# Gated attention and a token/channel mixer on one core: diagonal score blocks from 10 of 16 tiles, score runs of three, and DMA and buffer times in the planner

## The chip, the core and the metric

The kernel runs on one core of one Trainium2 chip. A core has TensorE (matmuls, with its own queue of weight loads), VectorE, ScalarE, GpSimd and SyncE; each takes its instructions in order, and they wait for one another by semaphores. DMAs are issued from SyncE's and GpSimd's queues here and carried out by 16 shared DMA engines. The metric is device time in microseconds. The core's span in the profile (first to last instruction) is a little shorter than that time.

## The reference

For each of 8 batches (sequence S = 3008, width 256, score width 64):

```python
scores = (1.0 / S) * np.matmul(z, z.transpose(0, 2, 1))
attn = np.maximum(scores, 0.0) ** 2
x = u * np.matmul(attn, v)
h = np.maximum(x.transpose(0, 2, 1) @ w_tok1, 0.0) @ w_tok2   # w_tok1 3008x256
y = x + h.transpose(0, 2, 1)
out = y + np.maximum(y @ w_ch1, 0.0) @ w_ch2                  # w_ch1 256x1536
```

Scores are z times its own transpose, so `attn` is symmetric: tile (k, q) is the transpose of tile (q, k). Inputs and output are float32; the kernel works in bf16 with float32 sums.

## The kernel before

**Tiles.** The sequence is cut into 24 key tiles of 128 rows (the last has 64 real rows, held twice), and both sequence axes into six blocks of four tiles (`NQ`, `NG`): 512 columns, the last 448. A score block (b, q, g) is four key tiles by one row block: 16 tiles of 128x128. `zT` holds z transposed, twice, in partitions 0 to 63 and 64 to 127, so that two score matmuls of 64 rows run side by side on the two halves of TensorE's array.

**Scores.** The unit of work is half a score block, two key tiles (`units`, L237). `score_run` (L314) issues one pair of matmuls for each unit into one PSUM slot `sc`; `relu` (L337) has ScalarE write relu(scale x scores) to a buffer `at`; `square` (L358) has VectorE square it in place. There are six `at` buffers, and three PSUM slots (the `ring`), which the mixer's products share.

**Symmetry.** In batch 0 all 36 blocks are computed. In batches 1 to 7 only blocks with g >= q are; for g > q, `flip` (L374) has SyncE issue one DMA transpose of all 16 tiles into a buffer `fl`, which serves as block (b, g, q). The `at` buffer is counted free by the planner (`release`, L382) when both uses are over, the flip's use being over when it is issued. Diagonal blocks (g = q) are computed in full, although each is symmetric in itself.

**Attention times v.** `Block`, `next_half` and `do_half` (L458) go through the six blocks of a row block, in two halves of 128 output columns each (`acc0`, `acc1`). For the half-filled last key tile the two halves run side by side as a pair of 64-row matmuls (`do_tails`, L435). `gate` (L492) multiplies by u, transposed by DMA (`turn_u`, L164), and `turn_x` (L514) transposes the result by DMA for the token mixer.

**The mixer** of a batch runs during the next batch's attention, as `Piece`s: `tok1` (L539, sums over the sequence, into PSUM tile `a_ps`), `tok2` (L559), `ch1` (L583, twelve hidden tiles by two, each evacuated by ScalarE or VectorE) and `ch2` (L617, twelve matmuls a piece; two pieces share a PSUM slot, the first opens it and the second closes it). `residual` (L635) adds on VectorE and SyncE stores the rows.

**What sets the order.** The order of every queue is written out by a planner in Python, in the same program. It keeps a clock for TensorE (`pe`), and for each of `act`, `dve` and `sp` the time from which it is free; `push` (L251) queues an operation with its busy time and its latency, `run_engines` (L269) issues those that could have started. The main loop (L819) picks what TensorE does next: a run of score units, a half of attention times v, or a mixer piece. A run of scores wants as many PSUM slots at once as it has units; `most` (L827) is three, or two while a mixer piece has a slot open. Modelled costs: 0.92 us for ScalarE on a pair, 0.61 for VectorE, 2.45 busy and 6.5 to landing for a flip, 1.25 and 5.5 for x and u transposes of the mixer. Changing TensorE between full and 64-row matmuls is priced at 0.095 us (`on_pe`, L290). `can_score` allows a unit if the number of live `at` buffers permits it.

**Loads** are hung on steps of attention times v by `at_group` (L748): z, v and u of what comes next and, in batch 0, the weights. They go through GpSimd's queue. u's transpose (`turn_u`) and z's (`turn_next_z`, L740) go through SyncE's; the planner counts 1.25 us of SyncE for z's and nothing for u's.

Of the kernel before, what the change touches and what calls it, by code (L numbers as in the profile page):

```python
# [13 lines left out]
P = 128  # L14
QW = 512
GK = 4
# [26 lines left out]
def kernel(  # L43
# [52 lines left out]
    def load_z(b, c):  # L96
        zs = sb.tile([P, GK, d_qk], BF16, tag="zs", name="zs", bufs=6)
        n = full_tiles[c]
        nc.gpsimd.dma_start(out=zs[:, :n, :], in_=rows_of(z[b], c))
        if n < GK:  # L100
            for r in range(2):
                nc.gpsimd.dma_start(
                    out=zs[r * TAIL:(r + 1) * TAIL, n, :], in_=last_rows(z[b]))
        return zs

    def turn_z(zs, zT, c, engine, tag="zr", bufs=2):
# [38 lines left out]
    def load_v(b, c):  # L145
        vt = sb.tile([P, GK, D], BF16, tag="v", name="v_sb", bufs=8)
        n = full_tiles[c]
        nc.gpsimd.dma_start(out=vt[:, :n, :], in_=rows_of(v[b], c))  # L148
        if n < GK:
            for r in range(2):  # L150
                nc.gpsimd.dma_start(
                    out=vt[r * TAIL:(r + 1) * TAIL, n, :], in_=last_rows(v[b]))
        vs[b, c] = vt

    def load_u(b, q):
        ur = sb.tile([P, QW // P, D], BF16, tag="ur", name="ur", bufs=2)
# [5 lines left out]
        urs[b, q] = ur  # L162

    def turn_u(b, q):  # L164
        ur = urs.pop((b, q))
        uT = sb.tile([P, QW // P, DT, P], BF16, tag="uT", name="uT", bufs=3)
        nc.sync.dma_start_transpose(
            out=uT.rearrange("p t h s -> p (t h) s"),
            in_=ur.rearrange("p t d -> p (t d)"))
        uTs[b, q] = uT  # L170

    def load_w_tok1(c):
        n = full_tiles[c]
        nc.gpsimd.dma_start(
            out=w_tok1_sb[:, c * GK:c * GK + n, :], in_=rows_of(moe_w_tok1, c))
        if n < GK:
            nc.gpsimd.memset(w_tok1_sb[TAIL:, KT - 1, :], 0.0)
            nc.gpsimd.dma_start(
                out=w_tok1_sb[:TAIL, KT - 1, :], in_=last_rows(moe_w_tok1))

    def load_w_tok2(c):
# [5 lines left out]
        ws[c] = st  # L187

    def order_w_tok2(c):
        st = ws.pop(c)  # L190
# [9 lines left out]
    def load_w_ch(part):  # L200
        if part < 2:
            nc.gpsimd.dma_start(
                out=w_ch1_sb[:, part, :], in_=moe_w_ch1[part * P:(part + 1) * P, :])
        else:
            h = CHT // 2
            c0 = (part - 2) * h
            nc.gpsimd.dma_start(
                out=w_ch2_sb[:, c0:c0 + h, :],
                in_=moe_w_ch2.rearrange("(cc c) d -> c cc d", c=P)[:, c0:c0 + h, :])

# [30 lines left out]

    free = {"act": 0.0, "dve": 0.0, "sp": 0.0}
    waiting = {"act": [], "dve": [], "sp": []}
    ring = [Done(0.0) for _ in range(3)]
    live = {"at": 0, "fl": 0, "xT": 0, "x": 0, "h2": 0, "us": 0}
    ROOM = {"at": 6, "fl": 10, "xT": 9, "x": 7, "h2": 8, "us": 2}
    FAR = 1e9

    def push(engine, ready, busy, lat, fn, first=0, room=(), done=None):  # L251
        op = Op(ready, busy, lat, fn, first, room, done)
# [16 lines left out]
    def run_engines(until):  # L269

        while True:
            best = next_op()
            if best is None or best[0][0] > until:
                return
            (start, _, _), e, op = best
            waiting[e].remove(op)
            free[e] = start + op.busy
            op.done.t = start + op.lat
            op.fn(op.done.t)

    def known(*events):
# [8 lines left out]
    def on_pe(start, kind, length):  # L290
# [4 lines left out]
        pe[0] = start + length  # L295
        return start, pe[0]


    ats, ready_at = {}, {}
    turned = {}  # L300
# [13 lines left out]
    def score_run(us, start):  # L314
        slots = sorted((d for d in ring if d.t is not None), key=lambda d: d.t)
        for unit in us:
            (b, q, g), pr = unit
            zT = zTs[b].rearrange("p t s -> p (t s)")
            W = widths[q]
            slot = slots.pop(0)  # L320
            ring.remove(slot)
            begin = max(start, slot.t, known(turned[b, q], turned[b, g]))
            begin, start = on_pe(begin, "half", column_time(W))
            sc = psum.tile([P, 2, QW], F32, tag="ps", name="sc", bufs=3)
            for r in range(2):
                k = g * GK + pr * 2 + r
                h = slice(r * d_qk, (r + 1) * d_qk)
                nc.tensor.matmul(  # L328
                    sc[:, r, :W], zT[h, k * P:(k + 1) * P], zT[h, q * QW:q * QW + W],
                    start=True, stop=True)  # L330
            if pr == 0:
                live["at"] += 1
            done = push("act", begin + 0.43, 0.92, 1.08,
                        lambda t, unit=unit, sc=sc: relu(unit, sc, t))
            ring.append(done)

    def relu(unit, sc, t):  # L337
        (b, q, g), pr = unit
        W = widths[q]
        if pr == 0:  # L340
            ats[b, q, g] = sb.tile([P, GK * QW], BF16, tag="at", name="at", bufs=ROOM["at"])
            ready_at[b, q, g] = []
        at = ats[b, q, g]
        pair = slice(2 * pr, 2 * pr + 2)
        if g > q and b > 0:

            view = at.rearrange("p (j i s) -> p j i s", i=GK, s=P)[:, :, pair, :]
            sv = sc.rearrange("p i (j s) -> p j i s", s=P)
        else:
            view = at.rearrange("p (i w) -> p i w", w=QW)[:, pair, :W]  # L350
            sv = sc[:, :, :W]
        nc.scalar.activation(view, sv, ACT.Relu, scale=inv_S)  # L352
        ready_at[b, q, g].append(
            push("dve", t, 0.61, 0.75, lambda t: square(unit, view, t)))
# [3 lines left out]
    def square(unit, view, t):  # L358
# [12 lines left out]
            attn = at.rearrange("p (i w) -> p i w", w=QW)  # L371
        blocks[b, q, g] = (Done(t), attn, "at", uses)

    def flip(b, q, g, at, uses, done):  # L374
        fl = sb.tile([P, GK, QW], BF16, tag="fl", name="fl", bufs=ROOM["fl"])
        live["fl"] += 1
        nc.sync.dma_start_transpose(
            out=fl.rearrange("p j (i s) -> p (j i) s", s=P), in_=at[:])
        blocks[b, g, q] = (done, fl[:, :, :], "fl", [1])
        release("at", uses)  # L380

    def release(name, uses):  # L382
        uses[0] -= 1
        if not uses[0]:
            live[name] -= 1


    class Block:
# [30 lines left out]
    def finished(blk, g):  # L419
        blk.parts[g] -= 1  # L420
        if not blk.parts[g]:
            _, _, name, uses = blocks.pop((blk.b, blk.q, g))
            release(name, uses)

    def block_ready(blk, g):
        e = blocks.get((blk.b, blk.q, g))
# [105 lines left out]
    def add_mixer(b):  # L532
# [134 lines left out]
                               lambda end, q=q: tok2(q, end)))  # L667
        def add_ch1(q, c2):
            h2_done[q, c2] = Done()
            tails.append(Piece(4 * column_time(widths[q]), [u_done[q]],  # L670
                               lambda end: ch1(q, c2, end),
                               room=("h2", "us") if c2 == 0 else ("h2",)))

        def add_ch2(q, half, i):
            tails.append(Piece(1.312, [h2_done[q, c2] for c2 in range(CHT // 2)],
                               lambda end: ch2(q, half, i, end), opens=i == 0, closes=i == 1))


# [58 lines left out]
    load_u(0, 0)  # L737
    load_u(0, 1)

    def turn_next_z(b, c, zs):  # L740
        turn_z(zs, zTs[b + 1], c, nc.gpsimd)
        free["sp"] = max(free["sp"], pe[0]) + 1.25
        turned[b + 1, c] = Done(pe[0] + 9.0)


# [47 lines left out]
    for c in range(NG):  # L793
        at_group(NG + 1 + 4 * c, lambda c=c: load_w_tok1(c))
        at_group(NG + 3 + 4 * c, lambda c=c: load_w_tok2(c))
        at_group(NG + 6 + 4 * c, lambda c=c: order_w_tok2(c))
    for part in range(4):
        at_group(2 * NG + 6 * part, lambda part=part: load_w_ch(part))
# [20 lines left out]
    while cur[0] is not None or heads or tails:  # L819
# [4 lines left out]
        blk = cur[0]  # L824


        most = 2 if opened[0] is not None else 3  # L827
        n = can_score(done_units, most)
        slots = sorted(d.t for d in ring if d.t is not None)
        n_now = min(n, len(slots))  # L830
        ts = FAR
        if n_now:
            at = max(t, known(*(turned[b, c] for (b, q, g_), _ in
                                units[done_units:done_units + n_now] for c in (q, g_))))
            ts = max([at] + [slots[i] - 0.1 - 0.216 * i for i in range(n_now)])
# [75 lines left out]
```

## Time and profile before

| what | value |
|---|---|
| time, median of 7 runs | 1190.19 us (1189.67 to 1196.6) |
| the profiled execution's own time | 1189.89 us |
| its span | 1188.1 us |
| TensorE busy | 1169.5 us, 98% |
| ScalarE, VectorE busy | 551.8 us (46%), 539.1 us (45%) |
| SyncE's DMA queue (q1), share of 16 DMA engines | 54.8% |
| GpSimd's DMA queue (q0) | 19.4% |
| flips issued, and other DMA transposes | 105, and 188 (48 u, 48 x, 48 mixer, 44 z) |

Busy time is the union of an engine's instructions. A TensorE row shows source line, output <- inputs, rows*columns of the array used (64*128 is one half of it), then partitions x elements. "Idle before" is how long an engine stood still before a group, with what ended the wait; a wait for several things is put down to the last. An instruction on SyncE's queue is not counted as busy; its duration is the issue of a DMA, and "landing" is from its start to the last completion. A DMA share above 1 means that transfers queue up.

### The profile page before, as it was taken

What the parts mean: (1) busy time and instruction counts of PE and PEld (TensorE: products, weight loads), DVE (VectorE), ACT (ScalarE), POOL (GpSimd) and SP (SyncE); (2) the same over time, 40 slices, a digit from 0 to 9 for tenths busy, and PEclk for the clock granted to TensorE, in tenths of its full rate; (3) what the DMA queues carried; (4) which work ended last, traced back from release to release, by engine and by line L of the source; (5) the groups of instructions that cost most, each with busy time, mean ns of one, the idle gap of its engine ahead of it and who ended that gap; (6) DMA issues with size and microseconds to landing.
All of it is one profiled execution on the core that took longest, in us unless ns stands there. A gap on an engine that the chain in (4) does not pass through costs nothing.

```text
span 1188.1 us, 17216 instructions
## 1 busy us (share of the span) xinstructions
PE 1169.5 (98%) x6998; PEld 632.0 (53%) x7091; DVE 539.1 (45%) x727; ACT 551.8 (46%) x577; POOL 145.9 (12%) x272
## 2 busy tenths in 40 slices
PE   8998999999999999999999999999999999999998
PEld 3334554654546545565455555455454654555666
DVE  5774643355443453425534255243642336512444
ACT  7886464426533264424635436344454445523222
POOL 2660011010011010110101101011011000000000
PEclk9999999999999999999999999999999999999999
DMA  8999667995598884997659976699757967542121
GB/s 144 168 175 197 122 116 139 179 156 107 109 163 149 148 137 103 158 187 128 118 103 172 153 126 121 132 164 150 141 101 135 192 125 132 106 104 47 52 80 61
DMA packets 437311, 157.46 MB, mean 133 GB/s; under 512 B 401200, under 2 KB 414832, under 8 KB 437232
## 3 DMA queue, kind: packets, MB, share of 16 engines
q1 hardware_dynamic: 409376, 123.66, 54.8%
q0 software_dynamic: 27344, 32.32, 19.4%
q8 instruction: 55, 0.90, 0.3%
q10 hardware_dynamic: 512, 0.38, 0.1%
q14 instruction: 24, 0.20, 0.1%
HBM read 65.40 MB, written 24.64 MB: 76 GB/s over the span
## 4 chain that ended last, share of the span: by engine, by line
PE 96%; ACT 1%; issue 1%; DMA 1%; DVE 1%; DVEq 0%; ACTq 0%
PE acc L415 41%; PE op L626 21%; PE hp L595 20%; PE sc L328 7%; PE a_ps L548 4%; PE h_ps L565 3%; ACT at L352 1%; DMA fl<-at 1%; DVE xT L571 0%; DMA zf<-in_z_dram 0%; PE zp L134 0%; DVE h2pre L610 0%; PE wp L142 0%; DVE zr L128 0%; DVE at L360 0%
## 5 line engine op out<-in xcount | busy, mean ns | idle before, releaser
L352 ACT ACTIVATE at<-sc 128x1024 bf16<-128x1024 f32 (+1 forms) x366 | 346.8, 1017 | 289.1 <-PE sc L328 280.6
L360 DVE TENSOR_TENSOR at<-at 128x1024 bf16<-128x1024 bf16 (+1 forms) x366 | 255.4, 702 | 295.8 <-ACT at L352 291.9
L415 PE MATMUL acc<-at,v_sb 128*128 128x512 bf16 (+3 forms) x1440 | 351.9, 378 | 1.5 <-issue 0.3
L415 PEld LDWEIGHTS <-v_sb 128*128 128x128 bf16 (+1 forms) x2304 | 210.6, 98 | 264.4 <-issue 62.8
L608 ACT ACTIVATE h2pre<-hp 128x1024 bf16<-128x1024 f32 (+1 forms) x198 | 198.2, 1004 | 313.9 <-PE hp L595 313.9
L626 PE MATMUL op<-w_ch_sb,h2pre 128*128 128x256 bf16 (+1 forms) x2304 | 273.9, 273 | 0.1
L595 PE MATMUL hp<-xT,w_ch_sb 128*128 128x512 bf16 (+1 forms) x1114 | 267.6, 374 | 2.3 <-DVE xT L571 0.4
L626 PEld LDWEIGHTS <-h2pre 128*128 128x128 bf16 (+1 forms) x2304 | 224.0, 98 | 57.3 <-issue 11.6
L415 PE MATMUL acc<-fl,v_sb 128*128 128x512 bf16 (+1 forms) x818 | 198.5, 370 | 1.4 <-issue 0.5
L595 PEld LDWEIGHTS <-w_ch_sb 128*128 128x128 bf16 x1152 | 112.6, 98 | 128.6 <-issue 1.3
L639 DVE TENSOR_TENSOR res<-op,u_sb 128x512 f32<-128x512 f32 x88 | 60.6, 689 | 151.9 <-PE op L626 151.9
L610 DVE TENSOR_SCALAR h2pre<-hp 128x1024 bf16<-128x1024 f32 (+1 forms) x90 | 108.8, 1208 | 42.6 <-PE hp L595 42.6
L504 DVE TENSOR_TENSOR xT<-acc,uT 128x512 bf16<-128x512 f32 (+1 forms) x96 | 63.4, 665 | 137.5 <-PE acc L415 127.6
L328 PE MATMUL sc<-zT 64*128 64x512 bf16 (+1 forms) x732 | 103.7, 379 | 1.9 <-DMA zT<-zr 0.9
L158 POOL DMA_DIRECT2D ur<-in_u_dram x48 | 26.0, 543 | 361.1 <-DMA uT<-ur 354.3
L110 POOL COPY zr<-zs 128x512 bf16<-128x512 bf16 x42 | 29.1, 692 | 290.2 <-DMA zT<-zr 289.5
L328 PEld LDWEIGHTS <-zT 64*128 64x128 bf16 x732 | 29.6, 94 | 58.4 <-issue 42.1
L571 DVE TENSOR_TENSOR xT<-xT,h_ps 128x1024 bf16<-128x1024 bf16 (+1 forms) x48 | 55.5, 1190 | 7.0 <-PE h_ps L565 7.0
L548 PE MATMUL a_ps<-x_sb,w_tok_sb 128*128 128x256 bf16 x384 | 46.9, 278 | 4.9 <-ACT at L352 4.9
L148 POOL DMA_DIRECT2D v_sb<-in_v_dram x48 | 25.8, 541 | 190.9 <-PE acc L415 190.7
L548 PEld LDWEIGHTS <-w_tok_sb 128*128 128x128 bf16 x384 | 37.5, 100 | 16.2 <-issue 9.0
L565 PE MATMUL h_ps<-w_tok_sb,a_sb 128*128 128x512 bf16 (+1 forms) x183 | 44.7, 374 | 0.6
(35 smaller groups left out, 115.7 us busy)
## 6 DMA issues: line engine op xcount, KB each, us to landing
out_dram<-res SPq DMA_DIRECT2D x88, 256.0 KB, 2.4
v_sb<-in_v_dram POOLq DMA_DIRECT2D x40, 256.0 KB, 4.9
ur<-in_u_dram POOLq DMA_DIRECT2D x40, 256.0 KB, 5.6
zs<-in_z_dram POOLq DMA_DIRECT2D x35, 64.0 KB, 3.9
fl<-at SPq DMA_TRANSPOSE x105, 4.5
v_sb<-in_v_dram POOLq DMA_DIRECT2D x8, 192.0 KB, 6.5
w_ch_sb<-in_moe_w_ch_dram POOLq DMA_DIRECT2D x4, 384.0 KB, 6.3
ur<-in_u_dram POOLq DMA_DIRECT2D x8, 192.0 KB, 3.6
```

The source lines that it names most:

```text
L328: nc.tensor.matmul(sc[:, r, :W], zT[h, k * P:(k + 1) * P], zT[h, q * QW:q * QW + W], start=True, stop=True)
L352: nc.scalar.activation(view, sv, ACT.Relu, scale=inv_S)
L360: nc.vector.tensor_mul(view, view, view)
L415: nc.tensor.matmul(o, vs[blk.b, g][rows, i, dh * P:(dh + 1) * P], rhs, start=first, stop=stop, skip_group_check=True)
L504: nc.vector.tensor_mul(xT[:, dh, :full * P].rearrange("p (t s) -> p t s", s=P), acc[:, :full * P].rearrange("p (t s) -> p t s", s=P), uT[: ...
L548: nc.tensor.matmul(st["a_ps"][:, th, :], w_tok1_sb[:, k, th * P:(th + 1) * P], x[:, :, i, :], start=(k == 0 and th == 0), stop=(k == KT - ...
L565: nc.tensor.matmul(h[:, dh, :W], st["a"][:, th, dh * P:(dh + 1) * P], w_tok2_sb[:, th, q * QW:q * QW + W], start=(th == 0), stop=(th == 1))
L595: nc.tensor.matmul(hp[:, r, :W], w_ch1_sb[:, dc, cc * P:(cc + 1) * P], xT[:, dc, :W], start=(dc == 0), stop=(dc == DT - 1))
L608: nc.scalar.activation(h2[:, :, :W], hp[:, :, :W], ACT.Relu)
L610: nc.vector.tensor_single_scalar(h2[:, :, :W], hp[:, :, :W], 0.0, AX.max)
L626: nc.tensor.matmul(op[:rows[i], i, :], st["h2", q, cc // 2][:, cc % 2, c0:c0 + rows[i]], w_ch2_sb[:, cc, :], start=(cc == 0 and i == 0), s ...
L639: nc.vector.tensor_add(res.rearrange("p i (h d) -> p i h d", d=P), op.rearrange("p i (h d) -> p i h d", d=P), us[:, :, half * 2:half * 2 + ...
```

## The change

1. **Diagonal blocks of batches 1 to 7.** Key tile i of a diagonal block is multiplied with columns from i x 128 on only: 512, 384, 256 and 128 columns, 10 tiles of 16. The first unit takes tiles 0 and 1 (one on each half of the array); the second takes 2 and 3, with tile 2 on the half that had tile 1. Each tile then has its own activation and its own square. Three DMA transposes on SyncE (three tiles, two, one) mirror what lies above the diagonal into the same `at` buffer: the first two after the square of the first unit, the last after that of the second. The block is ready when the planner's time for the last has passed.
2. **Score runs.** A run is three units, with an open mixer piece or without (`RING`); if scores are wanted and a mixer piece has a slot open, the closing piece goes first.
3. **`at` buffers by time.** `at_free` holds the planned time from which each buffer is free: the landing of its flip or the end of its last product with v. A run of scores is not planned to start more than 0.6 us ahead of the time when the buffers it needs are free.
4. **DMA sharing in the planner.** Each load adds 1.3 us (parts of it, or more, by size) to a time up to which loads are under way (`loading`); a transpose that falls into it takes up to twice as long (`shared`). u's transposes now count 1.25 us on SyncE (`on_sp`), z's 0.6.
5. **Weights of the channel mixer.** `ch1` and `ch2` pieces also need `w_done`, 16 us after their load was asked for.

```diff
         vs[b, c] = vt
+        loading(LOAD)
...
         uTs[b, q] = uT
+        on_sp(1.25)
...
+    def loading(us):
+        loads[0] = max(loads[0], pe[0] + 1.0) + us
+
+    def shared(start, us):
+        both = min(us, max(0.0, loads[0] - start))
+        loads[0] += both
+        return us + both
...
+    at_free = [0.0] * ROOM["at"]
+    RING = 3
...
-            free[e] = start + op.busy
-            op.done.t = start + op.lat
+            extra = shared(start, op.busy) - op.busy if e == "sp" else 0.0
+            free[e] = start + op.busy + extra
+            op.done.t = start + op.lat + extra
...
+    def triangle(b, q, g):
+        return q == g and b > 0
+
+    def parts(unit):
+        (b, q, g), pr = unit
+        if not triangle(b, q, g):
+            return [(r, 2 * pr + r, 0, widths[q]) for r in range(2)]
+        order = ((0, 0), (1, 1)) if pr == 0 else ((1, 2), (0, 3))
+        return [(r, i, i * P, QW) for r, i in order]
...
-            begin, start = on_pe(begin, "half", column_time(W))
+            cost = column_time(W)
+            if triangle(b, q, g):
+                cost = (column_time(QW), column_time(P))[pr]
+            begin, start = on_pe(begin, "half", cost)
...
-            for r in range(2):
-                k = g * GK + pr * 2 + r
+            for r, i, c0, c1 in parts(unit):
+                k = g * GK + i
                 h = slice(r * d_qk, (r + 1) * d_qk)
                 nc.tensor.matmul(
-                    sc[:, r, :W], zT[h, k * P:(k + 1) * P], zT[h, q * QW:q * QW + W],
-                    start=True, stop=True)
+                    sc[:, r, c0:c1], zT[h, k * P:(k + 1) * P],
+                    zT[h, q * QW + c0:q * QW + c1], start=True, stop=True)
             if pr == 0:
                 live["at"] += 1
-            done = push("act", begin + 0.43, 0.92, 1.08,
+                at_free.remove(min(at_free))
+            busy = 0.92
+            if triangle(b, q, g):
+                busy = (0.87, 0.43)[pr]
+            done = push("act", begin + cost + 0.21, busy, busy + 0.16,
                         lambda t, unit=unit, sc=sc: relu(unit, sc, t))
...
+        if triangle(b, q, g):
+            a3 = at.rearrange("p (i w) -> p i w", w=QW)
+            for r, i, c0, c1 in parts(unit):
+                nc.scalar.activation(
+                    a3[:, i, c0:c1], sc[:, r, c0:c1], ACT.Relu, scale=inv_S)
+            push("dve", t, (0.62, 0.36)[pr], (0.76, 0.5)[pr],
+                 lambda t: square_triangle(unit, t))
+            return
...
+    def square_triangle(unit, t):
+        (b, q, g), pr = unit
+        at = ats[b, q, g]
+        a3 = at.rearrange("p (i w) -> p i w", w=QW)
+        for r, i, c0, c1 in parts(unit):
+            nc.vector.tensor_mul(a3[:, i, c0:c1], a3[:, i, c0:c1], a3[:, i, c0:c1])
+        if pr == 0:
+            for j, busy in ((0, 0.55), (1, 0.4)):
+                push("sp", t, busy, 5.0, lambda t, j=j: flip_tiles(a3, j))
+            return
+        ats.pop((b, q, g))
+        done = push("sp", t, 0.3, 5.5, lambda t: blocks.update(
+            {(b, q, g): (done, flip_tiles(a3, 2), "at", [1])}))
+
+    def flip_tiles(a3, j):
+        nc.sync.dma_start_transpose(
+            out=a3[:, j + 1:, j * P:(j + 1) * P], in_=a3[:, j, (j + 1) * P:])
+        return a3
...
-        release("at", uses)
+        release("at", uses, done.t)
-    def release(name, uses):
+    def release(name, uses, t=0.0):
         uses[0] -= 1
+        uses[1:] = [max([t] + uses[1:])]
         if not uses[0]:
             live[name] -= 1
+            if name == "at":
+                at_free.append(uses[1])
...
-            tails.append(Piece(4 * column_time(widths[q]), [u_done[q]],
+            tails.append(Piece(4 * column_time(widths[q]), [u_done[q]] + w_done[:2],
...
-            tails.append(Piece(1.312, [h2_done[q, c2] for c2 in range(CHT // 2)],
+            tails.append(Piece(1.312, [h2_done[q, c2] for c2 in range(CHT // 2)] + w_done[2:],
...
+    def on_sp(us):
+        start = max(free["sp"], pe[0])
+        free["sp"] = start + shared(start, us)
...
-        free["sp"] = max(free["sp"], pe[0]) + 1.25
+        on_sp(0.6)
...
-        most = 2 if opened[0] is not None else 3
-        n = can_score(done_units, most)
+        n = can_score(done_units, RING)
...
+            new = sum(pr == 0 for _, pr in units[done_units:done_units + n_now])
+            if new:
+                ts = max(ts, sorted(at_free)[new - 1] - 0.6)
-        whole = n_now == most or (n_now and done_units + n_now == len(units))
+        whole = n_now == RING or (n_now and done_units + n_now == len(units))
-        hold = n >= most and lead <= 4
+        hold = n >= RING and lead <= 4
...
+        elif hold and opened[0] is not None and tm <= t + NOW and pieces is opened[0]:
+            pick = "mixer"
         elif hold and ta <= t + NOW:
             pick = "av"
```

More of the change, by code (lines that the diff above doesn't have):

```diff
@@ L103, in load_z @@
                     out=zs[r * TAIL:(r + 1) * TAIL, n, :], in_=last_rows(z[b]))
+        loading(LOAD / 4)
         return zs
@@ L162, in load_u @@
         urs[b, q] = ur
+        loading(LOAD)
     def turn_u(b, q):
@@ L179, in load_w_tok1 @@
                 out=w_tok1_sb[:TAIL, KT - 1, :], in_=last_rows(moe_w_tok1))
+        loading(LOAD)
     def load_w_tok2(c):
@@ L187, in load_w_tok2 @@
         ws[c] = st
+        loading(LOAD)
     def order_w_tok2(c):
@@ L209, in load_w_ch @@
                 in_=moe_w_ch2.rearrange("(cc c) d -> c cc d", c=P)[:, c0:c0 + h, :])
+        loading(LOAD * 1.5)
     zTs, vs, urs, uTs, xTs, xs, ws = {}, {}, {}, {}, {}, {}, {}
@@ L245 @@
     waiting = {"act": [], "dve": [], "sp": []}
-    ring = [Done(0.0) for _ in range(3)]
+    loads = [0.0]
+    def loading(us):
[4 more added lines that the diff above has]
+        return us + both
     live = {"at": 0, "fl": 0, "xT": 0, "x": 0, "h2": 0, "us": 0}
     ROOM = {"at": 6, "fl": 10, "xT": 9, "x": 7, "h2": 8, "us": 2}
+    at_free = [0.0] * ROOM["at"]
+    RING = 3
+    ring = [Done(0.0) for _ in range(RING)]
     FAR = 1e9
+    LOAD = 1.3
     def push(engine, ready, busy, lat, fn, first=0, room=(), done=None):
@@ L422, in finished @@
             _, _, name, uses = blocks.pop((blk.b, blk.q, g))
-            release(name, uses)
+            release(name, uses, pe[0] + 0.2)
     def block_ready(blk, g):
@@ L796, with ask_w_ch @@
         at_group(NG + 6 + 4 * c, lambda c=c: order_w_tok2(c))
+    w_done = [Done() for _ in range(4)]
+    def ask_w_ch(part):
+        load_w_ch(part)
+        w_done[part].t = pe[0] + 16.0
     for part in range(4):
-        at_group(2 * NG + 6 * part, lambda part=part: load_w_ch(part))
+        n = 2 * NG + 6 * part
+        at_group(n, lambda part=part: ask_w_ch(part))
     per_batch = 0.87 * NQ * (2 + CHT // 2) + 1.35 * 4 * NQ
```

## The prediction

> **What bounds the kernel now.** I read the page's busy shares and its chain first, then the TensorE timeline around one run of scores, then the one place where TensorE stands still, then the rows of the DMA transposes.
>
> ```profile
> PE 1169.5 (98%) x6998; PEld 632.0 (53%) x7091; DVE 539.1 (45%) x727; ACT 551.8 (46%) x577; POOL 145.9 (12%) x272
> ...
> PE 96%; ACT 1%; issue 1%; DMA 1%; DVE 1%; DVEq 0%; ACTq 0%
> ```
>
> TensorE is busy 98% of the span and carries 96% of the chain that ended last; VectorE and ScalarE stand idle more than half the time. So an edit pays if it takes TensorE time away, and costs if it makes TensorE wait. What counts on TensorE is the spacing of starts, since matmuls overlap. The next fence is its timeline (start, length, group): three score pairs between two halves of attention times v.
>
> ```profile
> 317.81 1.03 PE L415 MATMUL acc<-at,v_sb 128*128 128x512 bf16 x4
> 318.76 0.80 PE L328 MATMUL sc<-zT 64*128 64x512 bf16 x6
> 319.49 1.04 PE L415 MATMUL acc<-at,v_sb 128*128 128x512 bf16 x4
> ```
>
> Four full matmuls of 512 columns take 4 x 0.216 = 0.864 us, yet the scores start 0.95 us after them: going from 128 rows to the two 64-row halves costs 0.096. Six score matmuls (three pairs) take about 0.75 from first start to the next full matmul. In the trace's starts a pair repeats after 0.222 to 0.223 (both members start 4 ns apart), and the last pair before a full matmul takes 0.308 instead of 0.216, so the way back costs 0.092. A visit to half mode therefore costs 0.188 beside its work. Counted from the weight loads of L328, the 366 score pairs lie in 139 visits: 84 of three pairs, 54 of two, one of six.
>
> Adding up all starts against these spacings leaves only one wait of more than 1.1 us on TensorE in the whole span (some matmuls are missing from the records, and their 0.22 us are not waits):
>
> ```profile
> 98.72 7.24 DMA fl<-at
> ...
> 106.06 1.03 ACT at L352
> ...
> 107.14 2.91 PE a_ps L548 x13
> ```
>
> That is the chain; the timeline and the windows of the same place:
>
> ```profile
> 106.06 2.86 ACT L352 ACTIVATE at<-sc 128x1024 bf16<-128x1024 f32 x3 [5.55 <-DMA fl<-at]
> 107.14 3.24 PE L548 MATMUL a_ps<-x_sb,w_tok_sb 128*128 128x256 bf16 x16 [4.89 <-ACT at L352]
> ```
> ```profile
> 107.14:110.31 3.17, 3.17 (x16) 2.15 (x16) 2.06 (x3) 1.78 (x2) 0.00 (x0) 0.56 1.00 183
> 252.73:254.48 1.75, 1.75 (x18) 1.39 (x18) 1.30 (x3) 1.50 (x2) 0.00 (x0) 1.00 0.26 47
> ```
>
> ScalarE wants to write a score block into an `at` buffer that a transpose is still reading: issued at 98.72, landed at 105.96. The planner had counted the buffer free when the transpose was issued. TensorE waits behind it for a PSUM slot, 5.05 us beyond the normal spacing, and then runs at a granted clock of 0.56: the same sixteen matmuls that take 1.75 us at 252.73 take 3.17. The place costs 5.05 + 1.4 = 6.4 us.
>
> The DMA transposes (issue time on SyncE min/median/max in ns, then issue to landing), and what SyncE waits for:
>
> ```profile
> L111 SPq DMA_TRANSPOSE zT<-zr x44: 1189/1226/2071, 4.7 to 918.8; - x44
> ...
> DMA to landing us min/median/max: 2.4/4.0/13.1
> ```
> ```profile
> L377 SPq DMA_TRANSPOSE fl<-at x105: 1317/2025/6152, 92.7 to 1052.7; - x105
> ...
> DMA to landing us min/median/max: 4.2/4.5/8.7
> ```
> ```profile
> SPq L167 <- DMA ur<-in_u_dram: 57.5, 8, 12.0
> ```
>
> Four tiles (L111) hold SyncE for 1.19 us, sixteen (L377) for 1.32 when nothing is in the way: issue is nearly independent of size.
>
> **The change part by part.** All sums are against the profiled execution's own 1189.89 us (span 1188.1); the median of the seven runs, 1190.19, is 0.3 higher.
>
> *Ten of sixteen score tiles.* 42 blocks change (7 batches, 6 diagonal blocks). Before, two pairs: 2 x 0.223 = 0.446 us, or 2 x 0.195 where the row block has 448 columns. After, one half of the array gets 512 + 128 columns, the other 384 + 256. If the halves run on independently, 640 of 1024 columns: 0.446 x 0.625 = 0.279, a gain of 0.167 (0.111 in the 448-column block): 35 x 0.167 + 7 x 0.111 = 6.6 us. If the second pair starts only after the longer member of the first, 768 columns: 0.335, gains of 0.111 and 0.055, together 4.3. Every pair in this trace has equal members, so no row decides; a loss is excluded, since no column is added. I take the middle, -5.5.
> The Trainium skill ("TensorEngine Tiling (Array Packing)", Key Properties) says that tiles of the array work independently and may run their weight loads and matmuls in parallel. No run here shows that for unequal members; by that rule alone the term would be -6.6.
>
> *ScalarE and VectorE.* A pair's single activation becomes two, and likewise the square. ScalarE's rows (1024 columns 1.024 us, 896 0.917, 512 0.599) give 0.83 ns a column and 0.17 fixed: 512, 384, 256 and 128 columns cost 0.60 + 0.49 + 0.39 + 0.28 = 1.76 against 2.05, 12 us less in all. VectorE's rows (0.706 and 0.656 for 1024 and 896) give 0.39 ns a column and 0.31 fixed: 1.73 against 1.41, 13 us more. Both engines are idle for over half the span; on TensorE's path: 0.
>
> *Three small transposes per diagonal block, 126 in all.* 252 tiles of 128x128 join some 3008 (105 x 16, 144 x 8, 44 x 4), so queue 1 goes from 54.8% to about 59%: no bound by itself, but windows such as 200 to 225 us already show a DMA share of 1.11. On SyncE the planner prices the three at 0.55 + 0.4 + 0.3 = 1.25 us; by L111's row they cost 3 x 1.19 = 3.6. It also lowers a z transpose from 1.25 to 0.6, against a row of 1.19. What follows on the queue (flips, x, u, out) comes up to 2.4 us later than planned. Cover: the planner gives a flip 6.5 us to land (median 4.5), an x transpose 5.5 (4.0), so about 2 us is in hand. The last diagonal tile: planned 0.95 + 5.5 = 6.45 after the square, by the rows 2.4 + 4.0 = 6.4. And the blocks are early: from the last square of a diagonal block (L360) to the first gate of the row block before it (L504), which is about when its products with v begin, the 42 blocks have 20 us in the median; three have less than 4 (batch 1's first block 2.1), three more less than 10. So six of 42 lose their cover, and for them the planner has other blocks or mixer pieces. Bounds: 0; and each of the six waiting out 4.0 us, 24. Near the first, since 36 are covered: +1.5.
> The Trainium skill speaks against this step ("DMA: Bandwidth & Descriptors", Rules for kernel authors): small transfers should be coalesced, because under 64 KB one pays mostly overhead, and the pieces here are 96, 64 and 32 KB. Taken as a verdict, it would put the term at its upper bound and the whole at 1202.5. Against it stands the row of the leads: overhead that lies 20 us ahead of its reader is paid by nobody.
>
> *Runs over the whole ring.* `most` was 2 while a PSUM accumulation is open, now always 3, and the open piece is closed first. Best case 366 / 3 = 122 visits, 17 x 0.188 = 3.2 us less. Runs of two stay where few blocks are ahead, and a tail that meets no run is a visit of its own (13 were). I take 126: -2.4. Bounds -3.2 and, if waiting for three free slots makes as many extra tail visits as it saves, +1.
>
> *The `at` slots by time, and shared DMA time.* The planner now sees that the slot at 101.9 is taken until its transpose has landed, and puts other work there. Bounds: -6.4, the place gone; 0, it waits for something else. Late next is `x_sb` (issued 97.38, landed 102.97 in the trace), which the token-mixing piece behind the stall needs, 1.1 us after 101.9. And batch 1's first diagonal block, with its cover of 2.1 us, now comes two DMA landings later just here (DMA share 1.1 to 1.2). I take -3.5, a little over half. The weight waits (`w_done`) bind in batch 1 only, after the weights' 6.3 us landings: 0. `loading` issues nothing.
>
> Sum: 1189.9 - 5.5 - 2.4 - 3.5 + 1.5 = 1180.0.
>
> **The rivals.**
> 1. *The stall only moves.* DMA is full from 60 to 120 us (windows at 1.1 to 1.3), so blocks, slots and x all come late whatever the order. Against: x had landed at 102.97, and token mixing could have run for 4 us. Without the 3.5: 1183.5.
> 2. *Slower: late diagonal tiles.* The transposes queue behind one another and behind `turn_u`, which has held the queue for up to 12.0 us waiting for a load; a product with v that was planned for 6.45 us after the square then stops TensorE, which takes its work in order. For it: the issue price is out by a factor of three. Against: 20 us of cover in the median. The other terms give 11.4 us, so it cancels them at 0.27 us a block over the 42, and makes the kernel slower by 0.3% at 0.36. If twelve of them wait 2 us, half a landing: 1189.9 - 11.4 + 24 = 1202.5.
> 3. *The scores gain less than they say*: halves in step (-4.3), and no fewer visits (0). 1189.9 - 4.3 - 3.5 + 1.5 = 1183.6.
>
> **How the numbers follow.** Forecast 0.48, rival 1 0.20, rival 2 0.18, rival 3 0.14. About 0.3%, 3.6 us, is what a measurement of this kernel can tell from no change; so faster means under 1186.6. The forecast (0.47 of 0.48), most of rivals 1 and 3 (0.26 of 0.34) and the mildest of rival 2 (0.02) lie there: 0.75. Same: 0.10, from the ends of rivals 1 to 3. Slower: 0.15, the rest of rival 2 with a little of rival 1. The forecast's own range is 1174 (6.6, 3.2 and 6.4 all gained: 1173.7) to 1185. For eight in ten it reaches up into rival 2: 1173 to 1192.
>
> **What would show it.** Scores: the 64-row matmuls of a diagonal block would start within 0.28 us (independent) or 0.335 (in step), and TensorE's busy time would fall by 7 to 9 us. Visits: nearly all of three pairs, 122 to 130. The wait near 102 us and the clock of 0.56 after it would be gone. Transposes: issue rows of the small ones near 1.19 us, not 0.3 to 0.55; and no wait of `acc` (L415) for a DMA on `at`. I am wrong if such waits add up to over 5 us, if ScalarE waits for `at` buffers in every batch, or if TensorE goes idle at batch starts because the planner holds the scores back for slots.

## The result and the profile after

The changed kernel takes 1183.85 us (median of 19 runs) against 1191.75 for the kernel before on the same chips: ratio 0.9937, 95% interval 0.9925 to 0.9948, so 7.5 us less. The forecast was 1180.0, range 1173 to 1192. The profiled execution took 1183.67 us, with a span of 1181.9.

The page of the changed kernel, busy times and chain:

```profile
PE 1162.8 (98%) x6997; PEld 634.9 (54%) x7091; DVE 535.1 (45%) x818; ACT 522.9 (44%) x654; POOL 145.1 (12%) x272
...
PE 94%; DMA 2%; issue 1%; ACT 1%; SPq 1%; DVE 1%; POOL 0%; DVEq 0%; ACTq 0%; POOLq 0%
```

TensorE is still the bound and has 6.7 us less to do. Its share of the chain has fallen, though: DMA's is 2% where it was 1%, and SyncE's queue has come in with 1%. TensorE waits for more, not for less.

**The scores.** TensorE's timeline around one diagonal block:

```profile
480.55 0.39 PE L491 MATMUL acc<-at,v_sb 64*128 64x512 bf16 x2
480.77 0.43 PE L368 MATMUL sc<-zT 64*128 64x512 bf16 x4
481.14 0.82 PE L491 MATMUL acc<-at,v_sb 128*128 128x512 bf16 x3
```

The four score matmuls (512, 384, 256, 128 columns) and the way back to full mode take 0.37 us. In the trace's starts they come 0, 3, 166 and 216 ns after the first: the third starts when the 384 columns of its half are through, while the first, on the other half, is still running. Where another pair follows, it starts after 0.272 us. The 366 pairs lie in 124 visits (114 of three pairs), with 14 more for a tail alone: 138 visits, where there were 152.

**The wait.** The chain of the changed kernel where batch 1 begins:

```profile
93.90 3.80 SPq L592
...
97.76 1.22 SPq L443
...
99.03 8.67 DMA fl<-at
...
107.80 0.99 ACT at L392 x2
108.83 0.61 PE sc L368 x2
```

It is the same wait as before, somewhat later: ScalarE wants an `at` buffer that a flip is still reading. The first flip was issued at 92.66 us in the kernel before; now at 99.03, behind three small transposes (L443, two at 87.73 and one at 97.76), a u transpose and an x transpose whose issue took 3.80 us. TensorE's timeline, and the windows of 100 to 130 us and of the stretch at half clock:

```profile
104.86 0.28 PE L368 MATMUL sc<-zT 64*128 64x256 bf16 x2
108.83 0.61 PE L368 MATMUL sc<-zT 64*128 64x512 bf16 x2 [3.69 <-ACT at L392]
...
124.73 0.38 PE L491 MATMUL acc<-at,v_sb 128*128 128x512 bf16 x1 [1.01 <-DMA at<-at]
```
```profile
100.00:130.00 30.00, 25.02 (x138) 12.02 (x138) 14.55 (x20) 11.78 (x16) 2.64 (x5) 0.89 1.06 167
```
```profile
107.35:114.18 6.83, 5.13 (x19) 2.03 (x19) 1.78 (x5) 3.67 (x7) 0.00 (x0) 0.50 1.18 226
```

TensorE waits 3.9 us, then runs at a granted clock of 0.50 for 6.83 us, and 124.73 is the one place in the span where it waits for a small transpose. (Windows list TensorE, weight loads, VectorE, ScalarE and GpSimd busy, then clock, DMA share and GB/s.)

**Where the time went.** TensorE's time from first to last start splits into three: the nominal spacing of its matmuls; 0.094 us for each change between full and half mode; and the rest, which is waiting, its start-up and the loss to half clock. Some 90 matmul records are missing from some traces, these two among them; their spacings are put back under columns here, by the kernels whose records are complete.

| us | columns | mode changes | waits |
|---|---|---|---|
| before | 1133.9 | 28.6 | 20.2 |
| after | 1127.6 | 25.9 | 22.8 |
| difference | -6.3 | -2.7 | +2.6 |

Together -6.4, against -6.2 between the two profiled executions (1183.67 and 1189.89).

### The profile page after: what moved, and what is told of

It is laid out like the page before. It is cut to its first block, busy times and chain, and to the rows that moved or that the text cites. A ratio compares the mean times of both kernels' runs of the same rounds, so it can differ in the third digit from the quotient of the medians.

```text
span 1181.9 us, 17718 instructions
## 1 busy us (share of the span) xinstructions
PE 1162.8 (98%) x6997; PEld 634.9 (54%) x7091; DVE 535.1 (45%) x818; ACT 522.9 (44%) x654; POOL 145.1 (12%) x272
## 3 DMA queue, kind: packets, MB, share of 16 engines
q1 hardware_dynamic: 445664, 131.94, 60.6%
## 4 chain that ended last, share of the span: by engine, by line
PE 94%; DMA 2%; issue 1%; ACT 1%; SPq 1%; DVE 1%; POOL 0%; DVEq 0%; ACTq 0%; POOLq 0%
PE acc L491 40%; PE op L702 21%; PE hp L671 20%; PE sc L368 6%; PE a_ps L624 3%; PE h_ps L641 3%; ACT at L404 1%; DMA fl<-at 1%; DMA at<-at 1%; DMA ur<-in_u_dram 1%; SPq L592 0%; DVE xT L647 0%; DMA zf<-in_z_dram 0%; SPq L170 0%; PE zp L135 0%
## 5 line engine op out<-in xcount | busy, mean ns | idle before, releaser
L684 ACT ACTIVATE h2pre<-hp 128x1024 bf16<-128x1024 f32 (+1 forms) x191 | 191.4, 1008 | 374.4 <-PE hp L671 374.4
L491 PE MATMUL acc<-at,v_sb 128*128 128x512 bf16 (+2 forms) x1443 | 348.5, 379 | 2.6 <-DMA at<-at 1.0
L404 ACT ACTIVATE at<-sc 128x1024 bf16<-128x1024 f32 (+1 forms) x282 | 269.8, 1023 | 155.1 <-PE sc L368 153.7
L412 DVE TENSOR_TENSOR at<-at 128x1024 bf16<-128x1024 bf16 (+1 forms) x282 | 195.2, 699 | 193.1 <-ACT at L404 184.6
L702 PE MATMUL op<-w_ch_sb,h2pre 128*128 128x256 bf16 (+1 forms) x2304 | 270.0, 273 | 0.1
L491 PE MATMUL acc<-fl,v_sb 128*128 128x512 bf16 (+1 forms) x814 | 195.6, 370 | 1.9 <-issue 1.0
L686 DVE TENSOR_SCALAR h2pre<-hp 128x1024 bf16<-128x1024 f32 (+1 forms) x97 | 116.8, 1204 | 51.2 <-PE hp L671 51.0
L368 PE MATMUL sc<-zT 64*128 64x512 bf16 (+1 forms) x732 | 97.2, 365 | 5.3 <-ACT at L392 3.7
L392 ACT ACTIVATE at<-sc 128x512 bf16<-128x512 f32 (+3 forms) x168 | 60.6, 446 | 73.7 <-PE sc L368 68.7
L431 DVE TENSOR_TENSOR at<-at 128x512 bf16<-128x512 bf16 (+3 forms) x168 | 45.7, 325 | 49.6 <-ACT at L392 49.5
L111 POOL COPY zr<-zs 128x512 bf16<-128x512 bf16 x42 | 28.8, 687 | 266.5 <-DMA zT<-zr 266.1
L149 POOL DMA_DIRECT2D v_sb<-in_v_dram x48 | 25.8, 541 | 189.0 <-PE acc L491 188.8
```

Of the source, the lines that this page charges most:

```text
L368: nc.tensor.matmul(sc[:, r, c0:c1], zT[h, k * P:(k + 1) * P], zT[h, q * QW + c0:q * QW + c1], start=True, stop=True)
L392: nc.scalar.activation(a3[:, i, c0:c1], sc[:, r, c0:c1], ACT.Relu, scale=inv_S)
L412: nc.vector.tensor_mul(view, view, view)
L491: nc.tensor.matmul(o, vs[blk.b, g][rows, i, dh * P:(dh + 1) * P], rhs, start=first, stop=stop, skip_group_check=True)
L684: nc.scalar.activation(h2[:, :, :W], hp[:, :, :W], ACT.Relu)
L686: nc.vector.tensor_single_scalar(h2[:, :, :W], hp[:, :, :W], 0.0, AX.max)
```

## The experiments

**One part alone, one part undone.** Four kernels on one chip. `e_tri_alone` is the kernel before with the ten-tile blocks only. The others change the kernel after:

```diff
-        return q == g and b > 0
+        return False
```

is `e_notri`; `e_most2` takes the old run length back:

```diff
-        n = can_score(done_units, RING)
+        most = 2 if opened[0] is not None else 3
+        n = can_score(done_units, most)
...
-        whole = n_now == RING or (n_now and done_units + n_now == len(units))
+        whole = n_now == most or (n_now and done_units + n_now == len(units))
-        hold = n >= RING and lead <= 4
+        hold = n >= most and lead <= 4
...
-        elif hold and opened[0] is not None and tm <= t + NOW and pieces is opened[0]:
-            pick = "mixer"
```

and `e_noslots` drops the buffer times from the choice:

```diff
-            if new:
-                ts = max(ts, sorted(at_free)[new - 1] - 0.6)
```

> The kernel before with the ten-tile diagonal blocks alone; run length, buffer times, DMA sharing, weight waits and SyncE prices as before. Theory A (the score columns carry the gain: 35 blocks at 0.446 - 0.272 and 7 at 0.39 - 0.272, 6.9 us; the crowded start of batch 1 takes some back, about 2 us more than before): 1183 to 1187 beside 1190 to 1192. Theory B (the three small transposes cost as much as the columns give, and the planner's new times carry the gain): within 2 us of the kernel before, or slower.

> The changed kernel with full diagonal blocks; runs of three, buffer times and DMA sharing kept. Theory A: 14 visits to half mode fewer give 2.6 us, and without the small transposes the wait near 104 us is at most what it was before (6.4 us with the low clock): 1183 to 1189. If the wait is gone: the lower end. Theory B: like the changed kernel, 1182 to 1185.

> The changed kernel with the old rule for the length of score runs (two while a mixer piece is open). Theory A: visits go back from 138 to about 152 and the time rises by 14 x 0.188 = 2.6 us over the changed kernel, to about 1186. Rival: run length is worth nothing because the switch hides behind other waits: within 1 us of the changed kernel.

> The changed kernel without the planned times of the at buffers in the choice of score runs. Theory A (the wait near 104 us is the DMA queue's, the planner's time for the buffers missed it): within 1.5 us of the changed kernel. Rival: the buffer times do their work in every other place, and without them ScalarE waits for flips in several batches: 3 us or more above the changed kernel.

Measured against the kernel before (ratio, interval; visits; the three parts of the profiled execution as above):

| kernel | median us | ratio | visits | columns | changes | waits |
|---|---|---|---|---|---|---|
| e_tri_alone | 1193.89 | 1.0012 (0.9990 to 1.0034) | 152 | 1127.7 | 28.6 | 38.0 |
| e_notri | 1184.46 | 0.9920 (0.9882 to 0.9959) | 135 | 1133.9 | 25.4 | 16.9 |
| e_most2 | 1194.24 | 1.0008 (0.9985 to 1.0031) | 153 | 1127.6 | 28.8 | 31.3 |
| e_noslots | 1184.88 | 0.9931 (0.9902 to 0.9960) | 137 | 1127.5 | 25.8 | 21.6 |

The profiled execution of `e_tri_alone` was the slowest of its ten (1201.92), so its waits are at the high end; those of `e_notri` and `e_noslots` were the fastest of theirs, 1.1 and 2.6 us under the median. Where the text sets a kernel against the changed one in us, it takes medians, which were not measured side by side; by the ratios a difference can be up to 2.6 us other.

The columns do what they should in every kernel that has the ten-tile blocks, and yet those blocks alone gain nothing, and leaving them out of the changed kernel loses nothing that the intervals show. Theory A's figure for `e_tri_alone` (1183 to 1187) is wrong, and theory B's, within 2 us of the kernel before, holds: what shows in the time is longer runs together with the planner's new terms, and the waits that the ten-tile blocks bring eat their columns. Longer runs with the old planner were not run, so these two are not told apart. The waits and the chain of `e_tri_alone` show where the largest loss lies (there are others in this execution, such as 3.5 us for a z transpose near 500 us):

```profile
PE acc L488 <- DMA at<-at: 6.2, 2, 4.3
```
```profile
86.15 13.83 DMA ur<-in_u_dram
99.99 1.24 SPq L170
...
101.33 12.18 DMA fl<-at x2
...
113.61 1.03 ACT at L401
114.69 2.81 PE a_ps L621 x16
```

TensorE waited 6.2 us in two for the first three small transposes. They were issued at 88.7 to 91.2 us and took 10.9 to 14.3 us to land. SyncE then stood before u's transpose until its load had landed, 13.83 us after its issue, and the first flips came behind that. A product with v stopped by a late diagonal tile is the mechanism of rival 2, though here by landing and not by the queue alone; this planner prices the small transposes as the changed kernel's does, but knows nothing of loads. `e_notri`'s windows, at the same place as above, show what the start of batch 1 costs without small transposes:

```profile
100.00:130.00 30.00, 27.86 (x164) 13.53 (x162) 16.30 (x22) 12.70 (x15) 2.63 (x5) 1.00 1.11 184
```

2.1 us idle instead of 5.0, and no half clock. `e_notri` itself does not decide between its theories, whose ranges overlap there. `e_noslots` comes out in theory A's range, 1.0 us over the changed kernel: the buffer times are worth nothing that can be measured. But the reason is not theory A's, for in its profiled execution the wait is not there. Its TensorE timeline from 101 us:

```profile
101.18 5.40 PE L624 MATMUL a_ps<-x_sb,w_tok_sb 128*128 128x256 bf16 x48
106.42 1.03 PE L491 MATMUL acc<-at,v_sb 128*128 128x512 bf16 x4
108.16 1.33 PE L368 MATMUL sc<-zT 64*128 64x512 bf16 x6 [0.72 <-ACT at L392]
```

Its first flip is issued at 100.66, later than the 99.03 of the changed kernel, yet all 48 matmuls of token mixing run while ScalarE waits for it. The changed kernel runs 40 of them and then stands behind scores (104.86 above) with 8 left. `e_most2` was 10 us over the changed kernel (8.5 by the ratios) where theory A allowed 2.6; in the profiled executions 2.9 of it is mode changes and 8.5 are waits, most at the start of batch 1 (5.8 us idle at 104 us, 2.5 at 149, each with a half clock after it; another 1.7 is a half clock near 10 us).

**What the start of batch 1 waits for.** `e_tri2` leaves only batch 1's diagonal blocks full:

```diff
-        return q == g and b > 0
+        return q == g and b > 1
```

`e_wch_late` asks for the last two weight loads later:

```diff
-        n = 2 * NG + 6 * part
+        n = (2 * NG, 2 * NG + 6, 6 * NG + 4, 6 * NG + 6)[part]
```

`e_price` gives the planner the issue times that the trace shows:

```diff
-            for j, busy in ((0, 0.55), (1, 0.4)):
+            for j, busy in ((0, 1.2), (1, 1.2)):
...
-        done = push("sp", t, 0.3, 5.5, lambda t: blocks.update(
+        done = push("sp", t, 1.2, 5.5, lambda t: blocks.update(
...
-        on_sp(0.6)
+        on_sp(1.25)
```

and `e_noshare` lets `shared` return the plain time:

```diff
-        both = min(us, max(0.0, loads[0] - start))
-        loads[0] += both
-        return us + both
+        return us
```

> The changed kernel with full diagonal blocks in batch 1 too; ten tiles from batch 2 on. Theory A (the ten-tile blocks pay everywhere but at the crowded start of batch 1, where their transposes delay the flips): 6/7 of 6.9 us, that is 5.9, under the kernel without any ten-tile block, so 1177 to 1180. Rival (the small transposes cost as much as the columns give in every batch): 1183 to 1185.

> The changed kernel with the second half of the channel weights (two loads of 384 KB) asked for some 15 steps later, after batch 1 has begun. Theory A (loads and transposes share the DMA engines before batch 1, and the loads are what makes the flips land after 8 us): the wait near 104 us shrinks by 2 us or more, and the time is 2 to 5 us under the changed kernel. Rival (SyncE's own queue is what is late, by the issue of the small transposes and by u's wait for its load): within 1.5 us of the changed kernel.

> The changed kernel with the planner's SyncE price of the small transposes at 1.2 us each and of z's at 1.25. Theory (prices that are too low make the plan too hopeful at the start of batch 1): the wait near 104 us shrinks, 2 to 4 us under the changed kernel. Rival (the plan misses DMA landing, not issue): within 1.5 us of the changed kernel.

> The changed kernel without the doubling of transposes by loads in the planner. If the sharing is what keeps other batches free of waits: 2 us or more above the changed kernel. If it only matters at the start of batch 1, where the plan misses anyway: within 2 us of it.

| kernel | median us | ratio | visits | columns | changes | waits |
|---|---|---|---|---|---|---|
| e_tri2 | 1181.12 | 0.9905 (0.9884 to 0.9926) | 137 | 1128.4 | 25.8 | 16.4 |
| e_wch_late | 1188.13 | 0.9965 (0.9943 to 0.9986) | 137 | 1127.7 | 25.8 | 27.3 |
| e_price | 1181.52 | 0.9923 (0.9894 to 0.9952) | 138 | 1127.8 | 25.9 | 17.5 |
| e_noshare | 1186.31 | 0.9963 (0.9942 to 0.9984) | 137 | 1127.6 | 25.8 | 23.4 |

The profiled executions of `e_tri2`, `e_price` and `e_noshare` were the fastest of theirs, by 2.2 to 3.0 us under the median, that of the changed kernel lay at its median; so their waits are at the low end.

`e_tri2` has six sevenths of the columns and `e_notri`'s small waits (16.4 us against 16.9). So in these executions the ten-tile blocks cost no waits from batch 2 on, and its rival, that the small transposes cost as much in every batch, falls. Theory A's 1177 to 1180 is missed too, by 1.1 us: the profiled executions of `e_tri2` and `e_notri` are 5.2 us apart, but by the ratios `e_tri2` is only 1.8 us under `e_notri`, well within the intervals. Against the changed kernel the medians differ by 2.7 us, but the two intervals touch (0.9926 and 0.9925): a likely gain, not a shown one.

`e_wch_late` is 4.3 us slower than the changed kernel by the medians (the intervals just overlap), where theory A expected 2 to 5 faster and its rival no more than 1.5 either way. The loads had been moved on top of batch 1's flips: its DMA share from 100 to 130 us is 1.20 instead of 1.06, and TensorE is busy 23.94 of these 30 us. It speaks against moving loads there; whether fewer loads before batch 1 would help is left open. `e_price` kept TensorE busy through the place:

```profile
100.00:130.00 30.00, 30.00 (x177) 14.43 (x175) 16.43 (x28) 15.07 (x22) 2.93 (x6) 1.00 1.11 184
```
```profile
100.74 5.40 PE L624 MATMUL a_ps<-x_sb,w_tok_sb 128*128 128x256 bf16 x48
```

Its first flip is issued at 100.02, even later than the 99.03 of the changed kernel. Lateness of flips alone is therefore not the cost: as in `e_noslots`, the 48 matmuls of token mixing run without a break while the flips land. TensorE pays when the next thing in its plan depends on a flip that has not landed, as the scores at 104.86 of the changed kernel do. This is read from the profiled executions; no run changes this order alone. `e_noshare` is 2.5 us over the changed kernel, more than the 2 that its second theory allowed and within the first's figure; the intervals overlap. Its waits are where the second theory has them, at 104 to 109 us, with three of 0.4 to 1.2 elsewhere, so neither theory is shown.

**Is it the price?** The same three prices at 0.2 and at 2.0 us, prices together with `e_tri2`'s edit, and prices with the old run length.

> The changed kernel with all these SyncE prices at 0.2 us. If prices below the rows make the plan too hopeful: as the changed kernel or above, 1184 to 1189. If the price does not matter and the plan is a matter of luck: 1180 to 1190, with no order against 0.55, 1.2 and 2.0.

> The changed kernel with all these SyncE prices at 2.0 us, over what the rows show. If a plan that is careful about SyncE is what removes the waits: like prices of 1.2, 1180 to 1183. If 1.2 helped only because any edit makes another plan: anywhere from 1180 to 1190.

> The changed kernel with SyncE prices of 1.2 us a small transpose and 1.25 a z transpose, and full diagonal blocks in batch 1. If both edits act on the same waits at the start of batch 1, little adds up: 1179 to 1182, and batch 1's full columns cost 1 us against prices alone. If they act on different ones: 1176 to 1178.

> Prices of 1.2 us and the old rule for run length. Theory A (run length is worth its visits, about 15 x 0.188 = 2.8 us, and the rest of the 10 us that the old rule cost was the start of batch 1): 2 to 4 us above prices alone, 1183 to 1186. Rival (runs of two do harm of their own everywhere): 1189 or more.

| kernel | median us | ratio | visits |
|---|---|---|---|
| e_price_low (0.2) | 1194.31 | 1.0023 (0.9993 to 1.0053) | 136 |
| after (0.55, 0.4, 0.3; z 0.6) | 1183.85 | 0.9937 (0.9925 to 0.9948) | 138 |
| e_price (1.2; z 1.25) | 1181.52 | 0.9923 (0.9894 to 0.9952) | 138 |
| e_price_high (2.0) | 1197.78 | 1.0045 (1.0010 to 1.0080) | 137 |
| e_price_tri2 | 1182.30 | 0.9921 (0.9887 to 0.9954) | 137 |
| e_price_most2 | 1185.38 | 0.9950 (0.9924 to 0.9975) | 150 |

Both ends are slower than the kernel before or no faster, and both lie outside what either theory allowed (1194 against at most 1190, 1198 against at most 1190). So a change of price can cost 10 us or more; why it does is shown only in part. At 0.2 the planner takes small transposes and z's transposes (their price was lowered too) for done too early, as the waits of `e_price_low` say (in us, times, longest):

```profile
PE acc L491 <- DMA at<-at: 8.3, 7, 3.9
...
PE sc L368 <- DMA zT<-zr: 4.6, 2, 3.4
```

Ahead of the small transposes of the longest of these, a flip held SyncE for 7.21 us (from 112.57), so their own price is not the whole of it.

At 2.0 those waits are gone (1.2 us for a z transpose is left) and others come, for the x transposes that token mixing needs; the waits and the chain of `e_price_high`:

```profile
PE a_ps L624 <- DMA x_sb<-xT: 10.5, 3, 6.3
```
```profile
957.47 1.97 SPq L450
...
959.52 1.26 SPq L170
...
960.88 2.04 SPq L450
...
963.02 6.34 DMA x_sb<-xT
...
969.40 1.87 PE a_ps L624 x8
```

An x transpose is issued at 963 behind three other transposes and lands 6.34 us later. Why its queue was that full there (a flip at 941.95 had taken 11.2 us to issue) was not followed up. So it is not shown that a price over the row does harm by itself; another plan that happens to be worse is a rival that these runs leave. Between 0.55 and 1.2 the intervals show no difference.

`e_price_tri2` did not add up: its profile has a wait of 5.4 us at 103.87 again, at the first token-mixing piece, where `e_tri2` waits 1.5 us and `e_price` not at all. Edits which should not harm the start of batch 1 switch a wait of one to six microseconds there on or off. Which of them a given plan has, no run here lets one foresee. `e_price_most2` is 3.9 us over `e_price` by the medians (0.0027 by the ratios, 3.2 us), within theory A's 2 to 4, but the intervals overlap: it agrees with run length being worth its visits, and with most of the 10 us of `e_most2` having been the start of batch 1.

No kernel run here is shown to beat the changed one; `e_tri2` comes closest.

## Why the prediction was right, and where it was not

- **Columns** (-5.5, between 4.3 and 6.6): -6.3. The halves run independently, by the starts at 166 and 216 ns; the rule of the Trainium skill ("TensorEngine Tiling (Array Packing)", Key Properties), that tiles work independently, holds here for members of unequal length, and its -6.6 was nearer than the middle that I took. Rival 3 is excluded.
- **ScalarE and VectorE** (0 on the path): 0. ScalarE's four activations average 0.597 + 0.497 + 0.394 + 0.296 = 1.78 us, as worked out (1.76). VectorE's four squares take 0.423 + 0.371 + 0.288 + 0.217 = 1.30, not 1.73: a line through two rows as close as 896 and 1024 columns does not give the fixed cost.
- **Small transposes** (+1.5): the row held for the issue, and the cover held for the products with v. The new line's rows on SyncE:

```profile
L443 SPq DMA_TRANSPOSE at<-at x126: 1120/1196/3294, 87.7 to 1029.9; - x126
...
DMA to landing us min/median/max: 2.3/2.4/10.3
```

  They issue in 1.20 us as L111's row said, and land in 2.4, sooner than the 4.0 taken. TensorE waited for one of them, 1.2 us beyond the normal spacing. Queue 1 went from 54.8% to 60.6%, a little over the forecast 59. The 1202.5 that the prediction drew from the Trainium skill's rule on small transfers ("DMA: Bandwidth & Descriptors", Rules for kernel authors) was too high; of the three pieces only the smallest is under the rule's 64 KB. What the small transposes cost indirectly, by standing ahead of flips, is not in this +1.2; see the next term.
- **Run length** (-2.4): -2.7 in mode changes.
- **The `at` slots and shared DMA time** (-3.5): this is the step that failed. The wait moved instead of going, as rival 1 had it: 3.9 us at 104.86, 0.5 at 110.8, and a half clock that lasted 6.83 us instead of 3.41 and cost 5.13 / 2 = 2.6 instead of 1.4. That is 7.0 us where there were 6.4, so +0.6. The buffer times did not prevent it, and without them the time is the same (`e_noslots`, whose profiled execution does not even have this wait); what time the planner had for this flip is not on record. The runs allow another account: without small transposes (`e_notri`) waits fall from 20.2 to 16.9 us, 3.3 of the 3.5 that I booked, and with them they rise to 22.8. Counted so, the planner's terms came as forecast, and the small transposes were mis-sized, 5.9 us for 1.5, by what they do at the start of batch 1. Since the parts do not add, no run decides between the two. I had named what was crowded there (DMA share above 1, the first diagonal block with 2.1 us of cover) and still booked a gain. (DMA was full from 70 us on; the window of 60 to 70 us is at 1.00.)

By these steps the sum is -6.3 - 2.7 + 0.6 + 1.2 = -7.2; the remaining 0.8 us of waits in the profiled execution is start-up and small gaps. The whole came out within the range because the largest miss, 4.1 us, was partly made good by columns and runs, which is luck. The range says little besides, since the time before lay in it, and rival 1's 1183.5 came nearer than the forecast. Two of the signs named beforehand failed: TensorE's busy time fell by 6.7 us and not by 7 to 9, and the low clock after the wait did not go.

What the prediction did not see at all is that the parts do not add. Columns are worth 6.3 us on TensorE and nothing in the time when taken alone or taken out. With the planner as changed, the waits of `e_tri2` and of the changed kernel (16.4 and 22.8, in one execution each, the first the fastest of its kernel) put 6 us of that on the six blocks of batch 1, whose transposes go in front of that batch's flips. It is no law of those blocks: `e_price` has them and 17.5 us of waits, and `e_noslots` has them without the wait at this place.

## What to carry to other kernels

Where an in-order plan is full, cost a change stage by stage, and look first at the stage that has least in hand: there, cheap transfers placed in front of needed ones went with waits about as large as the columns saved in all batches. Look also at what the plan has for the engine while a late transfer lands: in `e_price` and `e_noslots` other work hid most of it. In the planner a price far below the row (0.2 us for 1.2) and one well above it (2.0) both lost here, while 0.3 to 0.55 and 1.2 were not told apart. Before a gain is put down to a part, run the part alone and the whole without it.

## What the runs showed of the hardware

- Two half-array matmuls of unequal length do not wait for each other: 512 and 384 columns start 3 ns apart, and the next matmul on the half with 384 starts at 166 ns, on the other at 216.
- A DMA transpose of one to three tiles of 128x128 holds SyncE for 1.12 us at least, a sixteen-tile one for 1.32. In `e_price_high` a flip took up to 11.5 us to issue and up to 21.6 to land; in the 13 us around its two longest issues the DMA share was 1.26 and 1.31.
- Waits on TensorE of 2.7 us (`e_noshare`) and 2.9 us (`e_wch_late`) were followed by a half clock of 3.41 us, of 3.9 us (after) by one of 6.83, while 1.8 us (`e_notri`) was not followed by any. The length of a wait does not decide it alone: 3.4 us at 816 us in `e_price_high` was not followed by any either, and 5.05 us in the kernel before by 3.41 only. The Trainium skill ("TensorE: Matmul & The Clock Gate", Part 1) has the clock decided over free-running windows of about 3.4 us, which agrees with the lengths 3.41 and 6.83; the waits here that were enough were shorter than a window.
